# Linear attention into an MLP on one core: q's turn split over two engines, a state term in a bank of its own, state sums in alternation, and another order for one wave's loads, turns and stores

## Chip, cores, metric

The kernel runs on one core of a Trainium2 chip. The metric is the time of one execution on the device in microseconds (us); the numbers of a kernel are medians over runs. Besides the runs there is one profiled execution, whose trace the views below are taken from.

## What is computed

```python
# attention: B=4 batches, H=8 heads, S=768 positions, D=64, blocks of 64
for b in range(nb):
    qb, kb, vb = (q[:, :, sl], k[:, :, sl], v[:, :, sl])
    intra = einsum('bhic,bhjc->bhij', qb, kb) * Dmask      # causal, lam**(i-j)
    intra = einsum('bhij,bhjd->bhid', intra, vb)
    inter = einsum('bhid,bhde->bhie', qb * lam_pow, kv_state)
    out[:, :, sl] = intra + inter
    kv_state = lam_block * kv_state + einsum('bhsd,bhse->bhde', kb * rev_pow, vb)
# MLP on x = out as 3072 rows of 512; w_in 512 x 2048, w_out 2048 x 512
h = x @ w_in
g = h * (1 / (1 + exp(-1.702 * h)))
result = g @ w_out                                          # 3072 x 512, float32
```

## The kernel before

The 768 positions of the four batches are worked through in six waves of 512 rows. Waves 0 and 1 are made differently from waves 2 to 5: each takes two batches (c = 0 and c = 1) and 256 positions of each, as two blocks of 128 positions interleaved in pairs. Waves 2 to 5 take 128 positions of all four batches. After a wave's attention its rows `xT` go through the MLP, whose products are done in a seven-product scheme (Strassen's) on sums of blocks: `product(w, n, ...)` for the second matrix, `in_product` for the first from wave 1 on.

The order of all engines' instructions is written out by hand (`tc.manual_schedule()`), so each engine's queue has the order of the program text. TensorE interleaves the MLP of one wave with the attention of the next. The steps of that interleaving have short names: `P50` is product 5 of the second matrix, first half of the tokens; `o` and `u` are the sums on VectorE (or from it) that finish two of the output blocks and store them; `p4h` is the last part of product 4. The change lies where wave 0's last products and wave 1's attention meet. Before, the order there on TensorE was: eight transposes of k (c = 0), `p4h`, eight transposes of q, `P50`, scores, the first state sum, `P51`, `d_even`, k's transposes (c = 1), `P30`, output sums, state sums, q's transposes (c = 1), `P31`, then wave 1's MLP with the scores of c = 1 in it.

What the names mean there:

- `turn_pe` (L235 on) transposes a cast k or q with TensorE into a PSUM bank `ps_t` and copies it to SBUF with the engine that it is given (one copy of 1024 columns, or of 512 with a group `g`). `turn_dma` (L246 on) does it by a DMA transpose issued by SyncE; waves 2 to 5 use it.
- `do_cast` multiplies a loaded k or q by its powers of lam into bf16, on VectorE or POOL (GpSimd). `cast_v` casts v, half on POOL and half on ACT (ScalarE) in wave 1.
- `d_scores` and `d_masks` make the scores in `ps_s` and mask them on VectorE. `d_out` sums the outputs of both row groups (A: partitions 0 to 63, Z: 64 to 127) in two banks, `oa` and `oz`, and then adds the second half of the state term, which is in row group Z, by `d_inter`.
- `d_even` makes the first half of the state term, in row group A, ahead of `d_out` in the bank that then serves as `oz`. A one-column copy on ACT (`seen`) stands between the two.
- `d_state` sums k'v for one row group; `d_one` does so for a batch's first row group in a new bank, and `d_keep` copies that to SBUF on ACT.
- `end(w, c)` runs `d_out`, the state sums, the copies to `xT` and the state's update. In `end(0, 1)` the first half of the state term already goes to a bank `ow` of its own; ACT copies two quarters of it to `term` and VectorE adds them.

PSUM has eight banks here in two rings: tag `a` with five and tag `mm` with three. A new tile takes the ring's next bank and waits until its last use is over. Bank X holds the running sum of products 1, 6, 5 and 3, and ACT or VectorE copies it out between them (L486, L484, L495, L500).

SyncE issues nearly all loads, stores and DMA transposes, in program order, and waits in that order for what each needs. Wave 2's loads are issued by `load(2, "kq")` behind the step `o`: k of both halves, then q of both, into one buffer each. Their casts on POOL and their turns come in the loop over wave 1's MLP, behind the stores of the steps `u` and `P31`.

Of the kernel before, what the change touches and what calls it, by code (L numbers as in the profile page):

```python
# [25 lines left out]
def kernel(  # L26
# [13 lines left out]
    nc = tc.nc  # L40
    f32 = mybir.dt.float32
    bf16 = mybir.dt.bfloat16
    B, H, S, D = q.shape
    P = 128
    NP = H // 2
# [27 lines left out]
    HF = 2  # L73
# [41 lines left out]
    A, Z = slice(0, 64), slice(64, P)  # L115
# [119 lines left out]
    def turn_pe(w, c, nm, copy=act_copy, g=None):  # L235
        x = cast[w, c, nm]
        rr = list(range(NP)) if g is None else [2 * g, 2 * g + 1]
        t = acc("ps_t", bf16, [P, len(rr), 2, P])
        for i, r in enumerate(rr):
            for a in range(2):  # L240
                nc.tensor.transpose(t[:, i, a, :], x[:, r, a, :], ident)  # L241
        if g in (None, 0):
            trans[w, c, nm] = work.tile([P, 2 * NP, P], bf16, tag=f"{nm}T{c}", bufs={"k": 1, "q": 2}[nm], name=f"{nm}T")
        copy(trans[w, c, nm][:, 2 * rr[0] : 2 * rr[0] + 2 * len(rr)], t.rearrange("p r a s -> p (r a) s"))
# [31 lines left out]

    kept = {}

    def d_state(w, c, t, bs):
        ks, vt = cast[w, c, "k"], v_sb[w % 2]  # L280
        for p in range(NP):
            for a in range(2):
                for j, js in enumerate((A, Z)):
                    h = 4 * (p // 2) + 2 * j + p % 2
                    nc.tensor.matmul(t[js, p, :], ks[bs, p, a, j * D : j * D + D], vt[bs, 2 * c + a, h, :],  # L285
                                     start=((bs is A or (w, c) in kept) and p + a == 0), stop=(a == 1), skip_group_check=True)

    states, whole = {}, {}

    def d_one(w, c, tag="a"):  # L290
        states[w, c] = t = acc("ps_kv", shape=[P, NP, D], tag=tag)
        d_state(w, c, t, A)

    def d_keep(w, c):
        nc.scalar.copy(kv_sb[1][:, 2 * w + c], states[w, c])
# [13 lines left out]
    def d_even(w, c, tag="a"):  # L309
        whole[w, c] = acc("ps_o", tag=tag)  # L310
        d_inter(w, c, whole[w, c], 0, True)
        nc.scalar.copy(seen, whole[w, c][:, 0, 0:1])
# [18 lines left out]
    def d_x(w, c, i, t, copy):  # L331
        n0 = (2 * c + i) * P
        copy(xT[w][:, :, n0 : n0 + P], t)
# [324 lines left out]
    with tc.manual_schedule():  # L658
        for x, i in ((k_pow, i_k), (q_pow, i_q)):
            nc.scalar.activation(x, ln_lam.unsqueeze(1).to_broadcast([P, 2, H]), EXP, scale=i)  # L660
        mk_pow(inv_pow, -1.0 * P)
        for j, rows in enumerate((A, Z)):
            nc.scalar.activation(blk_pow[rows].rearrange("p (r i) -> p r i", i=2),
                                 ln_lam[rows].rearrange("p (r j i) -> p r j i", i=2, j=2)[:, :, j, :], EXP, scale=1.0 * P)
        nc.scalar.activation(warm, q_pow[:, 0, 0:1], GELU)
        for nm, copies in (("k", (dve_copy, act_copy)), ("q", (act_copy, dve_copy))):
            for g in range(2):
                do_cast(0, 0, nm, nc.vector, g)
            for g in range(2):
                turn_pe(0, 0, nm, copies[g], g)  # L670
                fill(1 + g if nm == "k" else 1 - g)
        gate_pool(loaded[0, 0, "q"][0:1, H // 2, 0:1])
        load_w_in(0)
        load_one(0, 1, "v", v)
        cast_v(0, 0, (act_copy, act_copy))
        for pp in range(2):
            d_scores(0, 0, pp)
            d_masks(0, 0, pp)
        fill(3)
        do_cast(0, 1, "k", nc.gpsimd, 0)  # L680
        for j in range(1, len(IN_CH)):
            load_w_in(j)
        d_one(0, 0, "mm")
        d_keep(0, 0)
        turn_pe(0, 1, "k", act_copy, 0)
        oa, oz = d_out(0, 0, ("mm", "mm"))
        nc.scalar.copy(seen, oz[:, 3, P - 1 : P])
        do_cast(0, 1, "q", nc.vector, 0)
        do_cast(0, 1, "k", nc.vector, 1)
        do_cast(0, 1, "q", nc.vector, 1)  # L690
        turn_pe(0, 1, "q", act_copy, 0)
        d_inter(0, 0, oz, 0, False)
        turn_pe(0, 1, "k", act_copy, 1)
        d_state(0, 0, states[0, 0], Z)
        turn_pe(0, 1, "q", dve_copy, 1)
        d_x(0, 0, 0, oa, act_copy)
        d_x(0, 0, 1, oz, act_copy)
        cast_v(0, 1, (act_copy, pool_copy))
        for j in range(NCH):
            load_w_out(j)  # L700
        for pp in range(2):
            d_scores(0, 1, pp)
            d_masks(0, 1, pp, split=(1,) if pp else ())
        nc.gpsimd.affine_select(mask, mask, pattern=[[0, 1], [1, P]], channel_multiplier=-1, base=0,
                                compare_op=mybir.AluOpType.is_ge, fill=0.0)
        gate_sync(w_out_sb[1][0:1, 0, 0:2])
        load(1)
        mlp1_half(0, 0, 0)
        d_one(0, 1)
        d_keep(0, 1)  # L710
        act_copy(kv_sb[0][:, 0], states[0, 0])

        def scores(w, c):
            for pp in range(2):
                d_scores(w, c, pp)
            for pp in range(2):
                d_masks(w, c, pp)

        def end(w, c):
            oa, oz = d_out(w, c)  # L720
            t = acc("ps_kv", shape=[P, NP, D]) if w else states[w, c]
            if w == 0:
                ow = acc("ps_o", tag="mm")
                d_inter(w, c, ow, 0, True)
                term = work.tile([P, 2, P], f32, tag="sm", bufs=8, name="term")
                nc.scalar.copy(term, ow[:, 0::2])
                d_x(w, c, 0, oa, act_copy)
                n0 = (2 * c + 1) * P
                nc.vector.tensor_copy(xT[w][:, 1::2, n0 : n0 + P], oz[:, 1::2])
                nc.vector.tensor_tensor(xT[w][:, 0::2, n0 : n0 + P], term, oz[:, 0::2], op=ADD)  # L730
            d_state(w, c, t, Z)
            if w and c == 0:
                d_one(w, 1)
            if w:
                d_x(w, c, 0, oa, act_copy)
                d_x(w, c, 1, oz, act_copy if c else dve_copy)
            if w:
                nc.vector.tensor_tensor(kv_sb[0][:, 2 * w + c], kept[w, c], t, op=ADD)
            else:
                nc.scalar.copy(kv_sb[0][:, 2 * w + c], t)  # L740
            if w and c == 0:
                d_keep(w, 1)

        def steps(w, names):
            for s in names.split():
                one_step(w, s)

        end(0, 1)
        for c, fc in ((0, 2), (1, 0), (1, 2)):
            mlp1_half(0, c, fc)  # L750
        for fc in range(4, FFC):
            mlp1(0, fc)
            steps(0, {5: "I1 I2", 7: "I3", 9: "gl3 gl1 gl2 gl4", 11: "W01234", 13: "W11234"}.get(fc, ""))
        steps(0, "p1a gh3 gh1 p2a p7a W23124 p4a p1b p2b gh2 gh4 p7b p4b W33124 p1h p2h p7h")
        do_cast(1, 0, "k", nc.vector, 0)
        do_cast(1, 0, "k", nc.gpsimd, 1)
        do_cast(1, 0, "q", nc.vector)
        steps(0, "p6l p6h")
        turn_pe(1, 0, "k", act_copy)
        steps(0, "p4h o")  # L760
        turn_pe(1, 0, "q", act_copy)
        load(2, "kq")
        cast_v(1, 0, (pool_copy, act_copy))
        do_cast(1, 1, "k", nc.gpsimd)
        steps(0, "P50")
        scores(1, 0)
        d_one(1, 0)
        d_keep(1, 0)
        steps(0, "P51")
        d_even(1, 0, "mm")  # L770
        turn_pe(1, 1, "k", act_copy)
        do_cast(1, 1, "q", nc.gpsimd)
        cast_v(1, 1, (act_copy, pool_copy))
        steps(0, "P30")
        end(1, 0)
        steps(0, "u")
        turn_pe(1, 1, "q", act_copy)
        steps(0, "P31")
        halves = [(c, fc) for c in range(HF) for fc in HALVES]
        for i, (c, fc) in enumerate(halves):  # L780
            if i == 1:
                scores(1, 1)
                d_even(1, 1)
            if i == 3:
                end(1, 1)
            if i == 4:
                x_sums(1)
            mlp1_half(1, c, fc)
            if i == 2:
                steps(0, "I0")  # L790
            if i in (1, 2, 3, 4):
                nm = "kq"[(i - 1) % 2]
                do_cast(2, (i - 1) // 2, nm, nc.gpsimd)
                turn_dma(2, (i - 1) // 2, nm)
            if i == 6:
                load(2, "v")
        steps(1, STEPS[1])
        for w in range(ND, NW):
            steps(w, STEPS[w])
# [30 lines left out]
```

## Time and profile before

| | |
|---|---|
| median of 3 runs | 191.46 us (191.4 to 192.05) |
| profiled execution | 192.02 us, span 190.3 us |
| TensorE matmuls | 183.5 us busy, 96% of the span |
| VectorE | 152.5 us, 80% |
| ACT | 129.9 us, 68% |
| POOL | 53.2 us, 28% |
| clock granted to TensorE | 1.0 of full speed |
| DMA | 33.91 MB, mean 178 GB/s |

The span is what the trace covers; the execution's own time has 1.7 us around it. Busy time of TensorE counts matmuls whose ends are modelled and overlap. In the rows that follow PE is TensorE's matmuls, PEld its weight loads, DVE is VectorE, SPq SyncE's queue of DMA issues, and L with a number is a line of the kernel before.

### The profile page before, as it was taken

How to read it: one execution, taken by the hardware profiler on the slowest of the kernel's cores; microseconds unless marked ns; L12 is line 12 of the kernel's file. 1: busy time of each engine (PE TensorE's matmuls, PEld its weight loads, DVE VectorE, ACT ScalarE, POOL GpSimd, SP SyncE). 2: the span in 40 equal slices, each digit the busy share in tenths (PEclk: the TensorE clock that was granted, in tenths of full speed). 3: DMA queues.
4: the chain of work that ended last, by engine and by line, in shares of the span. 5: the costliest groups of instructions: out<-in, count | busy, mean ns of one | idle time of the engine just before them, and what ended most of it. 6: DMA issues, size and time to landing. Idle time of an engine off the chain costs nothing.

```text
span 190.3 us, 5531 instructions
## 1 busy us (share of the span) xinstructions
PE 183.5 (96%) x2295; PEld 151.5 (80%) x2295; DVE 152.5 (80%) x282; ACT 129.9 (68%) x242; POOL 53.2 (28%) x72
## 2 busy tenths in 40 slices
PE   7889999999999999999999999999999999999993
PEld 2457646888888888888888888888888888888882
DVE  2687697986687799879799879799789797888950
ACT  6677765157777986288895388885488876597611
POOL 5498100246449000294000393000492000000000
PEclk9999999999999999999999999999999999999999
DMA  5999999998987899987899465999355903300113
GB/s 156 303 259 183 205 206 207 314 320 238 238 218 177 194 225 232 227 187 137 200 237 241 156 165 119 232 235 256 134 138 124 209 1 114 110 5 0 55 56 113
DMA packets 90127, 33.91 MB, mean 178 GB/s; under 512 B 67958, under 2 KB 89974, under 8 KB 90102
## 3 DMA queue, kind: packets, MB, share of 16 engines
q1 hardware_dynamic: 84676, 28.84, 60.2%
q0 software_dynamic: 5424, 4.72, 15.2%
q8 instruction: 18, 0.29, 0.6%
q14 instruction: 7, 0.06, 0.1%
q10 hardware_dynamic: 2, 0.00, 0.0%
HBM read 27.26 MB, written 6.29 MB: 176 GB/s over the span
## 4 chain that ended last, share of the span: by engine, by line
PE 90%; SPq 3%; DMA 3%; ACT 1%; DVE 1%; issue 0%; ACTq 0%
PE ps_X L470 22%; PE ps_hX L561 17%; PE ps_V L470 10%; PE ps_hV L561 8%; PE ps_Q L470 6%; PE ps_h L420 6%; PE ps_h L408 5%; PE ps_hQ L561 4%; SPq L84 3%; DMA qf<-in_q_dram 3%; PE ps_s L341 2%; PE ps_o L396 2%; PE ps_o L383 1%; PE ps_o L322 1%; PE ps_t L241 1%; PE ps_kv L285 1%
## 5 line engine op out<-in xcount | busy, mean ns | idle before, releaser
L470 PEld LDWEIGHTS <-g_s 128*128 128x128 bf16 x384 | 37.0, 98 | 4.8
L580 ACT ACTIVATE g_sb<-h_sb 128x512 bf16<-128x512 f32 x54 | 32.6, 631 | 1.2 <-DVE h_sb L569 1.2
L561 PEld LDWEIGHTS <-w_in_t 128*128 128x128 bf16 x288 | 28.2, 98 | 3.3
L470 PEld LDWEIGHTS <-g_sb 128*128 128x128 bf16 x288 | 27.5, 98 | 4.1
L224 ACT COPY part<-ps_hX 128x512 f32<-128x512 f32 x32 | 18.3, 587 | 11.4 <-PE ps_hX L561 11.4
L470 PE MATMUL ps_X<-w_out_t,g_s 128*128 128x256 bf16 x192 | 23.1, 273 | 0.0
L561 PEld LDWEIGHTS <-w_in 128*128 128x128 bf16 x216 | 21.1, 98 | 2.4
L561 PE MATMUL ps_hX<-x_s,w_in_t 128*128 128x256 bf16 x144 | 21.6, 272 | 0.0
L447 DVE TENSOR_TENSOR g_s<-g_sb 128x1024 bf16<-128x1024 bf16 x24 | 16.2, 686 | 5.8 <-ACT g_sb L580 5.6
L212 POOL TENSOR_TENSOR qs<-qf,q_pow 128x512 bf16<-128x512 f32 x16 | 16.6, 1062 | 3.4 <-DMA qf<-in_q_dram 3.4
L212 POOL TENSOR_TENSOR ks<-kf,k_pow 128x512 bf16<-128x512 f32 x16 | 16.3, 1041 | 3.5 <-DMA kf<-in_k_dram 3.5
L653 POOL CAST behind_q<-x_s 1x1 f32<-1x1 bf16 x3 | 0.5, 177 | 57.9 <-DVE x_s L546 57.9
L221 DVE COPY part<-ps_hV 128x512 f32<-128x512 f32 x18 | 12.4, 687 | 5.3 <-PE ps_hV L561 5.3
L486 ACT COPY part<-ps_X 128x512 f32<-128x512 f32 (+1 forms) x13 | 6.7, 518 | 13.0 <-PE ps_X L470 13.0
L569 DVE TENSOR_TENSOR h_sb<-part,ps_hX 128x512 f32<-128x512 f32 x18 | 12.2, 680 | 2.6 <-PE ps_hX L561 2.1
L569 DVE TENSOR_TENSOR h_sb<-part,ps_hV 128x512 f32<-128x512 f32 x18 | 12.3, 684 | 1.0 <-PE ps_hV L561 1.0
L470 PE MATMUL ps_X<-w_out,g_sb 128*128 128x256 bf16 x96 | 12.6, 273 | 0.0
L470 PE MATMUL ps_Q<-w_out,g_sb 128*128 128x256 bf16 x96 | 12.5, 273 | 0.0
L224 ACT CAST v_sb<-vf 128x1024 bf16<-128x1024 f32 (+1 forms) x13 | 11.4, 885 | 1.4 <-DMA vf<-in_v_dram 1.3
L569 DVE TENSOR_TENSOR h_sb<-part,ps_hQ 128x512 f32<-128x512 f32 x18 | 12.2, 679 | 0.0
L580 ACT ACTIVATE g_sb<-ps_hX 128x512 bf16<-128x512 f32 x18 | 10.6, 588 | 1.8 <-PE ps_hX L561 1.8
L470 PE MATMUL ps_V<-w_out_t,g_s 128*128 128x256 bf16 x96 | 11.8, 273 | 0.0
(117 smaller groups left out, 355.8 us busy)
## 6 DMA issues: line engine op xcount, KB each, us to landing
kf<-in_k_dram SPq DMA_DIRECT2D x10, 512.0 KB, 6.6
qf<-in_q_dram SPq DMA_DIRECT2D x10, 512.0 KB, 6.7
vf<-in_v_dram SPq DMA_DIRECT2D x10, 512.0 KB, 6.0
out_dram<-o_sb SPq DMA_DIRECT2D x24, 128.0 KB, 2.4
out_dram<-o_sb SPq DMA_DIRECT2D x12, 256.0 KB, 2.8
w_out<-in_moe_w_out_dram POOLq DMA_DIRECT2D x4, 512.0 KB, 14.2
kf<-in_k_dram SPq DMA_DIRECT2D x4, 256.0 KB, 3.2
qf<-in_q_dram SPq DMA_DIRECT2D x4, 256.0 KB, 5.0
```

Of the source, the lines that this page charges most:

```text
L84: (nc.gpsimd if w == 0 and c and nm == "v" else nc.sync).dma_start(out=x[:, h : h + n], in_=src[2 * w + c, h : h + n, 0 : 2 * P, :].rearra ...
L212: eng.tensor_tensor(x.rearrange("p b (r i j d) -> p j (b r) i d", i=2, j=2, d=D)[:, j], f.rearrange("p h (a d) -> p (h a) d", a=2).rearran ...
L221: nc.vector.tensor_copy(out, in_)
L224: nc.scalar.copy(out, in_)
L408: nc.tensor.matmul(h, w_in_sb[j][:, kc, i * P : (i + 1) * P], xT[w][:, kc, :], start=(kc == 0), stop=(kc == KC - 1))
L420: nc.tensor.matmul(h[:, u, :], w_in_sb[j][:, kc, i * P : (i + 1) * P], xT[w][:, kc, cols], start=(kc == 0), stop=(kc == KC - 1))
L447: nc.vector.tensor_tensor(o, x, y, op=f)
L470: nc.tensor.matmul(bank[:, t], x[:, m, t * P : (t + 1) * P], y, start=((n in (1, 2, 7) or own) and t == ts[0] * last and m == 0), stop=(m ...
L486: nc.scalar.copy(part[w, n, t.start][:, t], bank[:, t])
L561: nc.tensor.matmul(bank[:, u], z[:, kc], y[:, kc], start=(n in (1, 2, 7) and u + kc == 0), stop=(kc == 1), skip_group_check=True)
L569: nc.vector.tensor_tensor(h, h_part[w, g, {2: 1, 5: 7, 4: 6}[n]], bank, op=ADD)
L580: nc.scalar.activation(g_of[w][:, a : b + 1 : b - a, 256 * i : 256 * i + 256], bank, GELU)
```

## The change

The turn of q (c = 0) of wave 1 becomes two groups, one copied by ACT and one by VectorE, and the step `o` moves behind it. In `end(1, 0)` the first half of the state term goes to its own bank `ow` behind `d_out`, with the copies that `end(0, 1)` has, and `d_even(1, 0)` goes. `d_state` takes several sums and alternates their matmuls; `end(1, 0)` runs c = 0's second row group and c = 1's first in one such call. Wave 2's loads come as k, q, k, q. The casts and turns of its first half move ahead of `u` and so ahead of the stores of `u` and `P31`; the second half's stay in the loop.

```diff
-    def d_state(w, c, t, bs):
-        ks, vt = cast[w, c, "k"], v_sb[w % 2]
+    def d_state(w, *sums):
+        vt = v_sb[w % 2]
         for p in range(NP):
             for a in range(2):
-                for j, js in enumerate((A, Z)):
-                    h = 4 * (p // 2) + 2 * j + p % 2
-                    nc.tensor.matmul(t[js, p, :], ks[bs, p, a, j * D : j * D + D], vt[bs, 2 * c + a, h, :],
...
+                for c, t, bs in sums:
+                    for j, js in enumerate((A, Z)):
+                        h = 4 * (p // 2) + 2 * j + p % 2
+                        nc.tensor.matmul(t[js, p, :], cast[w, c, "k"][bs, p, a, j * D : j * D + D],
+                                         vt[bs, 2 * c + a, h, :],
...
         def end(w, c):
             oa, oz = d_out(w, c)
             t = acc("ps_kv", shape=[P, NP, D]) if w else states[w, c]
-            if w == 0:
+            if c == (w == 0):
                 ow = acc("ps_o", tag="mm")
                 d_inter(w, c, ow, 0, True)
                 term = work.tile([P, 2, P], f32, tag="sm", bufs=8, name="term")
...
-            d_state(w, c, t, Z)
             if w and c == 0:
-                d_one(w, 1)
-            if w:
+                states[w, 1] = acc("ps_kv", shape=[P, NP, D])
+                d_state(w, (c, t, Z), (1, states[w, 1], A))
+            else:
+                d_state(w, (c, t, Z))
+            if w and c:
                 d_x(w, c, 0, oa, act_copy)
-                d_x(w, c, 1, oz, act_copy if c else dve_copy)
+                d_x(w, c, 1, oz, act_copy)
...
         turn_pe(1, 0, "k", act_copy)
-        steps(0, "p4h o")
-        turn_pe(1, 0, "q", act_copy)
-        load(2, "kq")
+        steps(0, "p4h")
+        turn_pe(1, 0, "q", act_copy, 0)
+        turn_pe(1, 0, "q", dve_copy, 1)
+        steps(0, "o")
+        for c in range(HF):
+            load_one(2, c, "k", k)
+            load_one(2, c, "q", q)
...
         steps(0, "P51")
-        d_even(1, 0, "mm")
         turn_pe(1, 1, "k", act_copy)
...
         end(1, 0)
+        for nm in "kq":
+            do_cast(2, 0, nm, nc.gpsimd)
+            turn_dma(2, 0, nm)
         steps(0, "u")
...
-            if i in (1, 2, 3, 4):
-                nm = "kq"[(i - 1) % 2]
-                do_cast(2, (i - 1) // 2, nm, nc.gpsimd)
-                turn_dma(2, (i - 1) // 2, nm)
+            if i in (1, 2):
+                do_cast(2, 1, "kq"[i - 1], nc.gpsimd)
+                turn_dma(2, 1, "kq"[i - 1])
```

More of the change, by code (lines that the diff above doesn't have):

```diff
@@ L277 @@
     kept = {}
-    def d_state(w, c, t, bs):
-        ks, vt = cast[w, c, "k"], v_sb[w % 2]
+    def d_state(w, *sums):
+        vt = v_sb[w % 2]
         for p in range(NP):
             for a in range(2):
-                for j, js in enumerate((A, Z)):
-                    h = 4 * (p // 2) + 2 * j + p % 2
-                    nc.tensor.matmul(t[js, p, :], ks[bs, p, a, j * D : j * D + D], vt[bs, 2 * c + a, h, :],
-                                     start=((bs is A or (w, c) in kept) and p + a == 0), stop=(a == 1), skip_group_check=True)
+                for c, t, bs in sums:
[3 more added lines that the diff above has]
+                                         vt[bs, 2 * c + a, h, :],
+                                         start=((bs is A or (w, c) in kept) and p + a == 0), stop=(a == 1),
+                                         skip_group_check=True)
     states, whole = {}, {}
@@ L291, in d_one @@
         states[w, c] = t = acc("ps_kv", shape=[P, NP, D], tag=tag)
-        d_state(w, c, t, A)
+        d_state(w, (c, t, A))
     def d_keep(w, c):
@@ L693 @@
         turn_pe(0, 1, "k", act_copy, 1)
-        d_state(0, 0, states[0, 0], Z)
+        d_state(0, (0, states[0, 0], Z))
         turn_pe(0, 1, "q", dve_copy, 1)
```

## The prediction, made before the result

> **What bounds the kernel now.** I read the busy times and the chain that ended last, then the waits from 57 us on, and then the timeline of the stretch that the change edits, engine by engine.
>
> ```profile
> PE 183.5 (96%) x2295; PEld 151.5 (80%) x2295; DVE 152.5 (80%) x282; ACT 129.9 (68%) x242; POOL 53.2 (28%) x72
> ```
>
> ```profile
> PE 90%; SPq 3%; DMA 3%; ACT 1%; DVE 1%; issue 0%; ACTq 0%
> ```
>
> TensorE is busy for 96% of the span and is 90% of the chain. From 57 us to the end the view of waits has two rows for TensorE's weight loads and none for its matmuls:
>
> ```profile
> PEld L341 <- issue: 1.7, 8, 0.2
> PEld L383 <- issue: 0.8, 4, 0.2
> ```
>
> Both are pauses of 0.2 us ahead of matmuls on half the array's rows, not waits for another engine. So what TensorE gains before 57 us arrives at the end undiminished, and so does what it loses. The change moves nothing before 39 us. The question is what TensorE gains between 39 and 53 us, and whether the moved DMAs still land ahead of their reader. TensorE's timeline there (start, length, what; in brackets the idle time before and who ended it):
>
> ```profile
> 40.68 1.03 PE L470 MATMUL ps_X<-w_out_t,g_s 128*128 128x256 bf16 x8
> 41.97 0.64 PE L262 MATMUL ps_s<-qT,kT 64*64 64x128 bf16 x32 [0.25 <-ACT qT L224]
> 42.41 0.48 PE L285 MATMUL ps_kv<-v_sb,ks 64*64 64x64 bf16 x16
> 42.82 1.05 PE L470 MATMUL ps_X<-w_out_t,g_s 128*128 128x256 bf16 x8
> 43.80 0.30 PE L304 MATMUL ps_o<-qT,kv 64*64 64x128 bf16 x4
> 44.03 0.62 PE L241 MATMUL ps_t<-ident,ks 128*128 128x128 bf16 x8
> 44.55 1.03 PE L470 MATMUL ps_X<-w_out,g_s 128*128 128x256 bf16 x8
> 45.51 0.64 PE L322 MATMUL ps_o<-sm,v_sb 64*64 64x128 bf16 x32
> 45.99 0.28 PE L304 MATMUL ps_o<-qT,kv 64*64 64x128 bf16 x4
> 46.10 0.67 PE L285 MATMUL ps_kv<-v_sb,ks 64*64 64x64 bf16 x32
> 46.70 0.62 PE L241 MATMUL ps_t<-ident,qs 128*128 128x128 bf16 x8
> 47.16 1.04 PE L470 MATMUL ps_X<-w_out,g_s 128*128 128x256 bf16 x8
> 48.03 1.04 PE L420 MATMUL ps_h<-xT,w_in 128*128 128x256 bf16 x8
> 48.99 0.64 PE L262 MATMUL ps_s<-qT,kT 64*64 64x128 bf16 x32
> ```
>
> The rows overlap, because a length includes the last matmul's way to PSUM; what counts is the distance between starts: 0.87 for a product of eight behind which full-array work follows (47.16 to 48.03), 0.46 for eight transposes (46.70 to 47.16).
>
> **The change part by part.** The other engines' timeline in that stretch, and two groups of copies:
>
> ```profile
> 40.90 1.02 ACT L224 COPY qT<-ps_t 128x1024 bf16<-128x1024 bf16 x1
> 41.80 0.63 ACT L224 CAST v_sb<-vf 128x512 bf16<-128x512 f32 x1
> 43.91 0.59 ACT L495 COPY part<-ps_X 128x512 f32<-128x512 f32 x1 [0.33 <-PE ps_X L470]
> 47.75 1.02 ACT L224 COPY qT<-ps_t 128x1024 bf16<-128x1024 bf16 x1
> 40.73 0.69 DVE L502 TENSOR_TENSOR o_sb<-part,ps_Z 128x512 f32<-128x512 f32 x1
> 41.34 0.68 DVE L502 TENSOR_TENSOR o_sb<-part,ps_Q 128x512 f32<-128x512 f32 x1
> 42.42 2.48 DVE L273 TENSOR_TENSOR sm<-ps_s,mask_d 128x512 bf16<-128x512 f32 x4 [0.41 <-PE ps_s L262]
> 41.41 2.04 POOL L204 TENSOR_TENSOR ks<-kf,kd_pow 128x512 bf16<-128x512 f32 x2 [0.89 <-DMA kf<-in_k_dram]
> 45.40 0.61 POOL L218 CAST v_sb<-vf 128x512 bf16<-128x512 f32 x1
> ```
>
> ```profile
> L224 ACT COPY qT<-ps_t 128x512 bf16<-128x512 bf16 x2 | 1.2, 586 | 1.2 <-PE ps_t L241 1.2
> L221 DVE COPY qT<-ps_t 128x512 bf16<-128x512 bf16 x2 | 0.8, 425 | 1.0 <-PE ps_t L241 1.0
> ```
>
> *q's turn by two engines.* The scores of c = 0 wait for ACT's copy of 1024 columns, 40.90 to 41.92. After: ACT copies half of them in 0.586, done at 41.49, which the first 16 matmuls need; VectorE takes the other half behind the Z sum, 41.34 to 41.77, ahead of the second 16. TensorE is then bounded by its own product, which ends at 40.68 + 1.03 = 41.71; a half-array row starts 0.07 ahead of such an end (43.80 against 42.82 + 1.05). Scores start at 41.64 instead of 41.97: 0.33 gained. ACT's cast of v moves up by 0.43 to end at 42.0, so the first state sum follows the scores at 41.64 + 0.44 = 42.08 and the next product, P51, 0.41 later at 42.49. On VectorE the Q sum (step o) now stands behind the copy: the sum starts at about 41.70 (the Z sum of 0.69 lets its successor start 0.08 early, so this copy too), the masks 0.61 behind it at 42.31 instead of 42.42. Masks gain only 0.1 and end at 42.31 + 2.48 = 44.79.
>
> *One row group's term in its own bank.* The four matmuls at 43.80 (d_even) and ACT's touch of their bank go. k's turn follows P51 at once, at 42.49 + 0.87 = 43.36, where it took 44.03 - 42.82 = 1.21. POOL has the last half of that k cast at 41.41 + 2.04 = 43.45, and only the last four transposes need it: no wait. The next product, P30, could start at 43.36 + 0.46 = 43.82. But it adds to bank X, and ACT must first copy P51's result out of it (L495). That copy started 0.04 behind P51's end (42.82 + 1.05 = 43.87), and P30 0.05 behind the copy's end (44.50). After: P51 ends at 43.54, the copy runs from 43.58 to 44.17, P30 starts at 44.22. So P30 stands 0.33 earlier, not 0.73: the second gain is swallowed there. The output sums follow 0.96 later, at 45.18; their masks ended at 44.79. The four matmuls come back behind them, at 0.11 (46.10 - 45.99), so the state sums could start at 45.18 + 0.48 + 0.11 + 0.11 = 45.88. What ACT and VectorE get for it, by wave 0's rows:
>
> ```profile
> L726 ACT COPY term<-ps_o 128x256 f32<-128x256 f32 x1 | 0.4, 372 | 0.2 <-PE ps_o L304 0.2
> L729 DVE CAST xT<-ps_o 128x256 bf16<-128x256 f32 x1 | 0.4, 425 | 0.7 <-PE ps_o L304 0.7
> ```
>
> That is 0.37 more on ACT, and on VectorE this copy and a sum of its shape in place of one copy of all 512 columns. Queued behind the term on ACT are the copy of x, two of the state, and q's second turn (47.75 to 48.77), for which the scores at 48.99 wait. ACT has the 0.33 from P51 and the 0.2 by which those scores trailed their copy to pay with, against 0.37. I take nothing, with up to 0.2 as the other end.
>
> *Sums alternate.* Alternating row groups, as the output sums do already, 32 matmuls take 0.48 (45.51 to 45.99). In sequence they took 0.60 (46.10 to 46.70), and the difference of 0.12 I take for the switch back to full rows, so alternating is worth nothing by these rows, at most 0.1. But the sums of both states now run together, and the seventh matmul already needs the second v, whose cast ends on POOL at 45.40 + 0.61 = 46.01. POOL has been busy since the landing at 41.41, which the change doesn't move. 26 matmuls are left then: 46.06 + 26 x 0.015 + 0.12 = 46.57 for q's turn instead of 46.70. From here on everything follows at the old distances: **0.13 gained**, rounded to 0.15.
>
> The page TensorEngine Tiling of the Trainium skill (Key Properties) says that independent tiles load weights and multiply in parallel, and that a change of tiling mode drains the array. By the first, two row groups in turn would halve the state sums and give some 0.2 more. This trace speaks against it: the output sums alternate and still take 0.48. The drain agrees with the 0.2 of issue above.
>
> *Wave 2's DMAs.* SyncE's and POOL's timeline before, one load's time to landing (the second k, issued at 45.51), and that of the turns:
>
> ```profile
> 41.45 2.73 SPq L508 DMA_DIRECT2D out_dram<-o_sb  x4
> 47.05 5.85 SPq L88 DMA_DIRECT2D qf<-in_q_dram  x2
> 53.00 4.23 SPq L508 DMA_DIRECT2D out_dram<-o_sb  x4
> 61.53 1.26 SPq L248 DMA_TRANSPOSE qT<-qs  x1
> 54.98 2.37 POOL L212 TENSOR_TENSOR qs<-qf,q_pow 128x512 bf16<-128x512 f32 x2 [3.38 <-DMA qf<-in_q_dram]
> 64.94 0.62 PE L341 MATMUL ps_s<-qT,kT 64*128 64x128 bf16 x16
> ```
>
> ```profile
> kf<-in_k_dram SPq DMA_DIRECT2D x1, 512.0 KB, 7.5
> ```
>
> ```profile
> DMA to landing us min/median/max: 2.7/2.7/4.5
> ```
>
> The loads are all issued by 52.90 in either order, and three turns took 57.23 to 61.53, 1.43 each. Before, the last turn starts at 61.53 and lands at 64.2, 0.7 ahead of its reader at 64.94, and TensorE waits for nothing. After, q of c = 0 is the second load; the second landed at 53.0. POOL casts it by 55.1 to 55.4, its turn is issued by 56.5 to 56.8, four stores take between 2.73 and 4.23 (the second with loads still queued), and the last turn starts at 60.7 to 62.5, landing at 63.4 to 65.2. The reader then comes at 64.8. With the loads landed by then I take stores near the low end: hidden, with 1 us in hand, and up to 0.4 lost at the other end. The stores that wait behind turns hold two of eight buffers, and those come round again only in wave 1's output sums, behind these scores.
>
> **Sum.** The profiled execution took 192.02 (span 190.3), 0.56 above the median of 191.46. After: 191.87 for it, and from the median 191.46 - 0.15 = **191.3**.
>
> **Rivals.**
> *Neither ACT's copy nor POOL's cast holds TensorE back.* Then both gains arrive: 0.33 and 0.40, less 0.11 for the four matmuls put back: 0.6, time 190.85. Against it: ACT stood idle for 0.33 ahead of its copy, so that start hangs on P51 and not on ACT's load; and the cast of v comes last in a queue that began with a landing.
> *The added copy on ACT becomes the wait*, and q's second turn ends late for its scores. At 0.2 beyond my sum the gain is gone: 191.5.
> *The last turn of wave 2 lands behind its reader.* If q of c = 0 lands only where the third load did, at 54.98, it is cast by 57.35 and turned by 58.8, stores go to 63.0, the last turn starts at 64.4 and lands at 67.1: TensorE stands 2.3 at its scores, 193.6. It decides where the last turn starts later than 62.1; from there each us is one us of time. For it: two turns now stand behind loads, and stores ahead of the last turns. Against: the cast before was late mainly because q was third in the queue.
> *The change moves instructions without any effect*: 191.46, inside the forecast's own range.
>
> **How the numbers follow.** The forecast with 0 to 0.3 gained (191.15 to 191.45) has 0.55, both gains 0.2, the added copy 0.1, the late turn 0.15, of which a third beyond 1 us. The runs shown spread from 191.4 to 192.05, so a range has to hold part of that: 190.7 to 192.2 leaves out the worst of the late turn and some of the spread. 0.5% is 0.96 us, about what a measurement of this kernel can tell from no change. No gain here reaches it alone, but half of the second case could with the spread of runs: faster 0.1. The late turn, with some spread, gives slower 0.08. Same: 0.82.
>
> **What would show it.** Right: scores of c = 0 at 41.6, P30 at 44.2 just behind ACT's copy, a wait for POOL's v inside the state sums, q's turn at 46.57, and no DMA wait at wave 2's first scores near 64.8. Wrong: P30 or the state sums without those waits, a DMA wait at those scores, or any wait of TensorE behind 57 us that the trace before lacks.

## The result and the profile after

The changed kernel takes 193.32 us (median of 14 runs) against 191.47 for the kernel before (14 runs): ratio 1.0085, 95% interval 1.0066 to 1.0103. The prediction was 191.3, in a range of 190.7 to 192.2, with 0.08 on slower. By that ratio it is slower by 1.6 us (the two medians lie 1.85 apart): outside the range, and by a way that is none of the prediction's cases. The profiled execution took 193.57 (span 191.8), 1.55 above that of before.

First the busy times and the chain that ended last, from the page of the kernel after:

```profile
PE 183.5 (96%) x2295; PEld 151.2 (79%) x2295; DVE 156.3 (82%) x284; ACT 129.6 (68%) x242; POOL 53.2 (28%) x72
PE 82%; DMA 6%; DVE 5%; POOL 2%; issue 1%; ACT 1%; SPq 1%; ACTq 0%; DVEq 0%
```

TensorE and POOL are as busy as before. VectorE is busy for 3.8 us more, with two instructions more, and has gone from 1% of the chain to 5%. The waits of TensorE's matmuls and weight loads from 50 to 64 us, where the kernel before has none on another engine (us in total, times, longest):

```profile
PE ps_hX L564 <- DVE x_s L549: 0.5, 1, 0.5
PE ps_hQ L564 <- DVE h_sb L572: 0.5, 1, 0.5
```
```profile
PEld L564 <- issue: 0.9, 2, 0.6
PEld L564 <- DVE x_s L549: 0.8, 1, 0.8
```

TensorE's timeline there, after:

```profile
57.97 0.60 PE L564 MATMUL ps_hQ<-xT,w_in 128*128 128x256 bf16 x4
59.06 0.61 PE L564 MATMUL ps_hX<-x_s,w_in_t 128*128 128x256 bf16 x4 [0.49 <-DVE x_s L549]
60.39 0.60 PE L564 MATMUL ps_hX<-x_s,w_in_t 128*128 128x256 bf16 x4
61.44 0.60 PE L564 MATMUL ps_hQ<-xT,w_in 128*128 128x256 bf16 x4 [0.46 <-DVE h_sb L572]
66.35 0.62 PE L344 MATMUL ps_s<-qT,kT 64*128 64x128 bf16 x16
```

and before, the same two places:

```profile
57.84 0.60 PE L561 MATMUL ps_hQ<-xT,w_in 128*128 128x256 bf16 x4
58.29 0.60 PE L561 MATMUL ps_hX<-x_s,w_in_t 128*128 128x256 bf16 x4
59.60 0.60 PE L561 MATMUL ps_hX<-x_s,w_in_t 128*128 128x256 bf16 x4
60.04 0.60 PE L561 MATMUL ps_hQ<-xT,w_in 128*128 128x256 bf16 x4
```

The distance from one group of four to the next is 0.44 to 0.45 before. After, it is 1.09 at the first place and 1.05 at the second: 0.64 and 0.61 lost. From q's turn of c = 1 (46.70 before, 46.61 after) to wave 2's first scores (64.94 and 66.35) the whole loss is 19.74 - 18.24 = 1.50, so these two places carry 1.25 of it. Another 0.22 goes just ahead of them, at the first group that reads an `x_s`: it starts 0.66 behind the group before it (56.88 to 57.54), where it was 0.44. Behind wave 2's first scores nothing differs: 1.41 late there, and a span longer by 1.5.

What TensorE waits for first is VectorE's `x_s` (the sums of x that the first products of wave 1 read). The second wait, for `h_sb`, follows from it: VectorE makes `h_sb` behind its last `x_s`, and the copy that leads up to it starts at 60.12 where it started at 58.04. VectorE's and POOL's timeline after:

```profile
52.70 0.29 DVE L540 TENSOR_TENSOR w_in_t<-w_in,w_in_t 128x256 bf16<-128x256 bf16 x1
53.02 1.17 DVE L540 TENSOR_TENSOR w_in_t<-w_in,w_in_t 128x256 bf16<-128x256 bf16 x1
54.11 1.13 DVE L540 TENSOR_TENSOR w_in_t<-w_in 128x256 bf16<-128x256 bf16 x1
55.16 1.13 DVE L540 TENSOR_TENSOR w_in_t<-w_in,w_in_t 128x256 bf16<-128x256 bf16 x1
57.85 1.16 DVE L549 TENSOR_TENSOR x_s<-x_s,xT 128x512 bf16<-128x512 bf16 x1
59.04 1.15 DVE L549 TENSOR_TENSOR x_s<-xT,x_s 128x512 bf16<-128x512 bf16 x1
52.99 2.10 POOL L212 TENSOR_TENSOR qs<-qf,q_pow 128x512 bf16<-128x512 f32 x2 [1.56 <-ACT xT L224]
55.05 2.15 POOL L212 TENSOR_TENSOR ks<-kf,k_pow 128x512 bf16<-128x512 f32 x2
57.64 2.27 POOL L212 TENSOR_TENSOR qs<-qf,q_pow 128x512 bf16<-128x512 f32 x2 [0.44 <-PE ps_hX L564]
```

and VectorE's before:

```profile
53.51 0.28 DVE L537 TENSOR_TENSOR w_in_t<-w_in,w_in_t 128x256 bf16<-128x256 bf16 x1
54.83 0.42 DVE L546 TENSOR_TENSOR x_s<-x_s,xT 128x512 bf16<-128x512 bf16 x1
55.29 1.15 DVE L546 TENSOR_TENSOR x_s<-xT,x_s 128x512 bf16<-128x512 bf16 x1
```

The same instruction takes 0.29 until 52.99 and 1.13 to 1.17 from then on, for as long as POOL casts: one VectorE sum per POOL instruction (2.10 / 2 = 1.05). Before, POOL had nothing to do from 51.6 to 54.98, since it waited for q as the third load, and the eight w_in_t sums ran in that gap. After, q is the second load, and its cast starts at 52.99, in the middle of them. The `x_s` that TensorE waits for ends at 57.85 + 1.16 = 59.01 where it ended at 54.83 + 0.42 = 55.25: 3.76 later. It was needed at 58.29 before, so 3.04 of slack were there, and 0.7 is missing. Of the 3.76, 2.50 come from the w_in_t sums alone (last end 56.29 against 53.79). A sum with one input in PSUM is not held up: the masks take 0.68 in both kernels, and the sum `kv` (L743, L738 before) takes 0.41 beside a cast (56.22 after) and 0.41 with POOL idle (53.72 before).

### The profile page after: what moved, and what is told of

Read it like the earlier page. It is cut to its first block, busy times and chain, and to the rows that moved or that the text cites. A ratio compares the mean times of both kernels' runs of the same rounds, so it can differ in the third digit from the quotient of the medians.

```text
span 191.8 us, 5533 instructions
## 1 busy us (share of the span) xinstructions
PE 183.5 (96%) x2295; PEld 151.2 (79%) x2295; DVE 156.3 (82%) x284; ACT 129.6 (68%) x242; POOL 53.2 (28%) x72
## 4 chain that ended last, share of the span: by engine, by line
PE 82%; DMA 6%; DVE 5%; POOL 2%; issue 1%; ACT 1%; SPq 1%; ACTq 0%; DVEq 0%
PE ps_X L473 22%; PE ps_hX L564 16%; PE ps_V L473 10%; PE ps_hV L564 8%; PE ps_Q L473 6%; PE ps_h L411 5%; PE ps_hQ L564 4%; DMA vf<-in_v_dram 4%; DMA qf<-in_q_dram 2%; PE ps_s L344 2%; PE ps_o L399 2%; PE ps_h L423 2%; DVE w_in_t L540 2%; DVE sm L273 1%; DVE x_s L549 1%; PE ps_o L386 1%
## 5 line engine op out<-in xcount | busy, mean ns | idle before, releaser
L473 PE MATMUL ps_X<-w_out,g_s 128*128 128x256 bf16 x96 | 11.6, 272 | 0.2 <-ACT part L498 0.2
```

The source lines that it names most:

```text
L473: nc.tensor.matmul(bank[:, t], x[:, m, t * P : (t + 1) * P], y, start=((n in (1, 2, 7) or own) and t == ts[0] * last and m == 0), stop=(m ...
```

## The experiments

**Theory A:** POOL's casts hold up VectorE's sums whose two inputs lie in SBUF, and the new order of loads puts a cast onto the w_in_t sums. **Rivals:** the DMA transposes ahead of the stores do it; the edits to wave 1 cost time; a late turn of wave 2.

**Only the order of the loads**, in the kernel before.

```diff
-        load(2, "kq")
+        for c in range(HF):
+            load_one(2, c, "k", k)
+            load_one(2, c, "q", q)
```

> The kernel before, with wave 2's loads as k q k q and nothing else of the change. Theory A (POOL's cast of q, now second to land, starts near 53 us and holds up VectorE's sums on two SBUF tensors): VectorE's w_in_t sums after 53 us take 1.1 us each instead of 0.3, TensorE waits for x_s near 58 us, 192.9 to 193.4. Theory B (the DMA turns, issued at 52.9 in the changed kernel, slow VectorE): turns start at 57 us here, so no loss, 191.5. Theory C (the edits of wave 1 cost it): 191.5.

Ratio 1.0083 (1.006 to 1.0106), 193.52 against 191.93: the loss of the whole change comes from these three lines. VectorE's and TensorE's timeline in this kernel:

```profile
52.62 1.13 DVE L537 TENSOR_TENSOR w_in_t<-w_in,w_in_t 128x256 bf16<-128x256 bf16 x1
59.21 0.60 PE L561 MATMUL ps_hV<-x_s,w_in_t 128*128 128x256 bf16 x4 [1.68 <-DVE x_s L546]
```

Five sums from 52.62 on take 1.02 to 1.13 each, and TensorE stands 1.68 for `x_s`. In this kernel the first DMA transpose starts only at 56.14, when three of the five sums are over, so the transposes are not what holds them.

**Only the edits to wave 1** (split turn, own bank, alternating sums); loads, casts and turns of wave 2 as before.

> Wave 1's edits alone (q's turn split, own bank, alternating sums); loads k k q q, casts and turns where they stood before. Theory A and theory B: 191.2 to 191.4, a gain of 0.1 to 0.2, with VectorE's w_in_t sums at 0.3 us each. Theory C: the loss stays, 193.3.

Ratio 1.000 (0.9977 to 1.0024). All eight w_in_t sums take 0.28 to 0.33, and TensorE waits for no `x_s`. The edits to wave 1 cost nothing, and gain nothing that can be told.

**One POOL cast of the kernel before, done twice.**

```diff
-            for j in range(2):
+            for j in (0, 1, 0, 1) if (w, c, nm) == (2, 0, "k") else (0, 1):
```

> The kernel before, with POOL's cast of wave 2's first k done twice (two more instructions of 1.05 us, in POOL's idle time from 51.6 to 53.7 us); no DMA moves. Theory A: VectorE's w_in_t sums from 51.9 us on are held up to 1.1 us each while POOL casts, 192.5 to 193.3. Theory B and theory C: 191.5.

Ratio 1.0195 (1.0152 to 1.0237): two instructions of 1.05 on an engine that is busy for 28% of the span cost 4 us. The extra casts run until 53.52, and sums beside them take 0.46 and 1.02. But in the traced execution q's own cast also starts earlier, at 53.94 where the kernel before had 54.98, and POOL then casts until 60.39; four more sums take 1.02 to 1.15 there, and TensorE waits 1.68 and 0.62 for `x_s`. So the trace doesn't tell how much of the loss is the extra casts' own. That there is one, the times tell: all six executions (194.04 to 196.71) lie above the longest of the 23 of the kernel before (193.12). It is more than expected, and a part of it is the clock, by the view of windows (busy of PE, PEld, DVE, ACT, POOL with counts; granted clock; DMA share; GB/s):

```profile
58.00:59.00 1.00, 0.00 (x0) 0.00 (x0) 1.00 (x3) 0.53 (x2) 1.00 (x2) 1.00 1.10 251
60.00:61.00 1.00, 0.57 (x6) 0.27 (x3) 0.97 (x2) 0.00 (x0) 0.39 (x1) 0.94 0.71 160
61.00:62.00 1.00, 0.81 (x4) 0.58 (x5) 0.96 (x3) 0.00 (x0) 0.00 (x0) 0.50 1.07 240
63.00:64.00 1.00, 1.00 (x7) 0.69 (x6) 0.03 (x1) 0.89 (x2) 0.00 (x0) 0.50 0.40 88
```

From 61 to 64 TensorE got half its clock, and its groups of four stand 0.83 to 0.85 apart instead of 0.44. Four of the six executions have a mean clock of 0.989 to 0.991 (195.97 to 196.71), the other two 1.0 (194.04 and 195.21): against the median of 191.93 those two lose 2.1 and 3.3 us without it.

**The cure: the changed kernel with the eight sums moved away from wave 2's casts.** The sums of step I0 go into two gaps on VectorE, four ahead of `end(1, 0)` and four behind `u`; `in_sums` gets an argument for it, which isn't shown.

```diff
         steps(0, "P30")
+        in_sums(0, (0,))
         end(1, 0)
...
         steps(0, "u")
+        in_sums(0, (1,))
...
-            if i == 2:
-                steps(0, "I0")
```

> The changed kernel, with the eight w_in_t sums of group 0 moved into VectorE's idle stretches at 44.8 and 47.8 us, ahead of POOL's casts of wave 2. Theory A: only the x_s sums still meet POOL's casts (1.15 us each), and they end in time: 191.1 to 191.4. Theory B: the same x_s sums meet the turns, and some loss may stay, 191.3 to 192. Theory C: 193.3.

Ratio 0.9985 (0.996 to 1.0009): the loss is gone, with loads, casts and turns of the change all in place. `x_s` still meets POOL, but has time now:

```profile
54.29 1.16 DVE L549 TENSOR_TENSOR x_s<-x_s,xT 128x512 bf16<-128x512 bf16 x1
55.48 1.15 DVE L549 TENSOR_TENSOR x_s<-xT,x_s 128x512 bf16<-128x512 bf16 x1
```

It ends at 56.63, and from 50 to 64 us TensorE's matmuls wait for no engine. It isn't shown to be faster than the kernel before: the interval reaches over 1. The new place isn't free of POOL either. Two of the four sums ahead of `end(1, 0)` meet wave 1's casts: one takes 1.02 beside q's, and this one starts 0.12 behind POOL's copy of v, which has a single input in SBUF and takes 0.67:

```profile
44.89 0.69 DVE L540 TENSOR_TENSOR w_in_t<-w_in 128x256 bf16<-128x256 bf16 x1
```

**Does any work on POOL hold VectorE up, or only work that reads SBUF?** The kernel before, with four memsets on POOL behind k's first cast, into a tile that is overwritten later.

```diff
                 do_cast(2, (i - 1) // 2, nm, nc.gpsimd)
+                if i == 1:
+                    for g in (0, 1, 0, 1):
+                        nc.gpsimd.memset(trans[1, 0, "k"][:, 4 * g : 4 * g + 4], 0.0)
```

> The kernel before with four extra memsets on POOL behind its first cast of wave 2's k, from about 51.6 us on, where POOL was idle until q's landing at 54.98 and VectorE made the w_in_t sums in 0.28 each; nothing reads what they write before it is written again. Theory A in its narrow form (only a POOL instruction that reads from SBUF holds up a VectorE sum with two inputs from SBUF): the sums stay at 0.28 to 0.3 and the time stays at the level of before, 0.2% at most. Wide form (any POOL instruction does): sums beside the memsets take as long as a memset, 0.6 or more, and if the memsets cover all eight sums, x_s ends 2 or more us later and TensorE waits up to 1.5: 192.5 to 193.5. If the memsets run past 54.98, q's cast and with it the last x_s start later by that much in both forms.

Ratio 0.9997 (0.9978 to 1.0016): the narrow form holds. The traced execution is a long one (194.89, where the median is 191.85), so only what lies side by side in it is read:

```profile
52.09 1.92 POOL L796 MEMSET kT<- 128x512 bf16 x4
53.26 0.28 DVE L537 TENSOR_TENSOR w_in_t<-w_in,w_in 128x256 bf16<-128x256 bf16 x1
54.52 2.24 POOL L212 TENSOR_TENSOR qs<-qf,q_pow 128x512 bf16<-128x512 f32 x2 [0.52 <-DVE w_in_t L537]
54.72 1.14 DVE L537 TENSOR_TENSOR w_in_t<-w_in 128x256 bf16<-128x256 bf16 x1
```

Beside a memset a sum takes 0.28; beside a cast, half a microsecond later, 1.14. The page SBUF — State Buffer of the Trainium skill (Who interferes with whom) says just this: a VectorE instruction with two SBUF inputs contends with a GpSimd instruction that reads SBUF, not with one that only writes, and the one that comes second waits for the whole instruction of the other. The traces agree in all three points. On the third: the `x_s` of the kernel before that starts at 54.83, ahead of POOL's cast, takes 0.42 and the cast 2.37, where the casts behind it take 2.05.

**The changed kernel with the loads as before** (k k q q), turns still ahead of the stores. This also comes near the prediction's rival of the late turn, which needs q of c = 0 to land where the third load did, at 54.98, and the last turn to start later than 62.1.

> The changed kernel with wave 2's loads in the order k, k, q, q as before; casts and turns of the first half stay ahead of the stores. Theory A: q of c = 0 lands as third load at about 55, POOL is idle from 51.6 to 55, VectorE's eight w_in_t sums run at 0.3 each and x_s is in time; the loss of the changed kernel (1.6) is gone: 191.3 to 191.7, as far as the second turn isn't late. The prediction's rival of the late turn: q is cast by 57.4, turned by 58.8, four stores take until about 62, the last turn starts at 63 to 64.4 and lands at 65.6 to 67.1, behind its reader at 64.8 to 65: TensorE waits 0.8 to 2.3 at wave 2's first scores, 192.3 to 193.8. If neither is so (the loads' order is not what hurts), the time stays at the changed kernel's 193.3 with w_in_t sums of 1.1.

Ratio 1.0013 (0.9985 to 1.0041): the loss goes with the order of the loads alone.

```profile
53.11 0.28 DVE L540 TENSOR_TENSOR w_in_t<-w_in,w_in_t 128x256 bf16<-128x256 bf16 x1
54.06 2.42 POOL L212 TENSOR_TENSOR qs<-qf,q_pow 128x512 bf16<-128x512 f32 x2 [2.88 <-DMA qf<-in_q_dram]
61.99 1.26 SPq L248 DMA_TRANSPOSE qT<-qs  x1
64.54 0.75 PE L344 MATMUL ps_s<-qT,kT 64*128 64x128 bf16 x16
```

The last w_in_t sum is over when q is cast. The first DMA transpose is issued at 51.84 here, and the sums beside it still take 0.28, so the transposes ahead of the stores hold none of them up. The last turn starts at 61.99, earlier than the 63 to 64.4 expected, because q landed by 54.06 and the four stores took 2.63, the low end of the prediction's bounds. That is 0.1 short of the rival's own condition. With 2.7 to its landing the turn is there at 64.69, while the scores that start at 64.54 are under way: they take 0.13 longer than after (0.75 against 0.62), and the next product starts 0.68 behind them instead of 0.56. The view of waits names nothing for so short a time; that it is the turn is an inference. So the rival came to its edge here and cost about 0.1; a turn that starts later was not tried.

**v first on POOL**, on top of the cure: the second half of v (c = 1) is cast ahead of q, so that the state sums need not wait for it.

```diff
-        do_cast(1, 1, "q", nc.gpsimd)
         cast_v(1, 1, (act_copy, pool_copy))
+        do_cast(1, 1, "q", nc.gpsimd)
```

> The changed kernel with the eight sums for the next wave's first product moved as in the run before (into VectorE's gaps around wave 1's c = 0), and on POOL the cast of the second half of v (c = 1) ahead of the cast of q (c = 1). Theory A (the loss is VectorE's two-input sums held up by POOL's casts; the wave-1 edits gain what was worked out): the state sums no longer wait for POOL's v, 0.44 in the run before; q's cast ends 0.6 later, but its turn comes behind all state sums, so about 0.1 to 0.2 is gained, 191.5 to 191.8, hardly above what can be told. Rival (POOL's casts of c = 1 bound wave 1 from the landing on): q's cast then ends later than its turn wants it, TensorE waits for POOL's q in place of POOL's v, and nothing is gained: the distance from POOL's start on k (c = 1) to q's turn stays 5.2, time 191.8 to 192.0.

A miss for both: ratio 1.0103 (1.0074 to 1.0132), 193.82. Its trace was of the shortest run (192.29) and showed 0.41 and 0.57 of new waits, so the same kernel was run again for a second trace:

> The same kernel as the run with the sums moved and v cast ahead of q on POOL, for a second trace: its times were 192.3 to 194.7 and the trace was of the shortest. If the 1.5 that its trace did not show lie in wave 1 (q's later cast lengthens TensorE's wait at q's turn, and VectorE's sums meet POOL's q cast), a trace of a run near 193.8 has q's turn of c = 1 at 8.5 or more behind k's turn of c = 0 (8.06 in the first trace); if they lie at wave 2, the distance from k's turn to wave 2's first scores grows (26.73 in the first) with q's turn unmoved and a wait of TensorE near x_s or those scores.

193.66, ratio 1.0097 (1.0058 to 1.0136), traced at 193.02:

```profile
45.91 1.12 DVE L540 TENSOR_TENSOR w_in_t<-w_in,w_in_t 128x256 bf16<-128x256 bf16 x1
48.12 0.38 ACT L301 COPY half<-ps_kv 128x256 f32<-128x256 f32 x1 [1.60 <-DVE kv L743]
44.13 0.67 POOL L218 CAST v_sb<-vf 128x512 bf16<-128x512 f32 x1 [1.31 <-DVE sm L273]
44.76 2.13 POOL L204 TENSOR_TENSOR qs<-qf,qd_pow 128x512 bf16<-128x512 f32 x2
46.95 0.40 PE L241 MATMUL ps_t<-ident,qs 128*128 128x128 bf16 x4 [0.65 <-POOL qs L204]
49.46 0.64 PE L262 MATMUL ps_s<-qT,kT 64*64 64x128 bf16 x32 [0.37 <-ACT qT L224]
```

POOL stands 1.31 ahead of v. The releaser named is VectorE's masks, but v's load was issued at 37.7 and took 6.3 to land by the profile's count, which is 44.0: v comes last of the loads, and POOL, put in front of it, idles while q lies ready. TensorE then waits for q in two steps (0.31 and 0.65) and for ACT's copy of it. q's turn stands 46.95 - 38.27 = 8.68 behind k's, as expected for a longer run. The rival was right in kind (POOL's q takes the place of POOL's v) and far too low in size. ACT's copy is late for the reason that this document is about: POOL's casts of v and q now lie beside the moved sums, three of the first four take 0.58, 1.12 and 1.12, VectorE's `kv` behind them starts 9.36 behind k's turn (8.43 in the cure), and ACT stands 1.60 for it ahead of q's copy. The last of the other four takes 1.14 beside the cast of wave 2's k, so the masks come late too, and TensorE stands 0.29 for them. From k's turn to wave 2's first scores it is 27.56 (26.73 in the first trace, 26.22 in the cure, 25.65 in the kernel before), and 0.62 of the 0.83 more than in the first trace lies at q's turn (8.68 against 8.06).

**The edits to wave 1, the split turn alone and two pairs**, on the kernel before. A single execution of the split turn alone took 190.43; it was then run 12 times, with the two pairs beside it.

> The kernel before with only q's turn (wave 1, c = 0) copied by two engines and step o behind it. By the prediction's steps: scores of c = 0 start 0.33 earlier beside k's turn than before, the product behind the first state sum as well, k's turn of c = 1 too, and the product P30 follows ACT's copy of bank X 0.33 earlier; with no alternation of the sums there is no wait for POOL's second v, and q's turn of c = 1 comes 0.3 earlier: 191.2. Rival (POOL's casts bound this stretch): POOL's q or v holds q's turn, which comes 0.1 earlier at most: 191.4. One look can't tell those times apart; the trace can.

> Again the kernel before with only q's turn (wave 1, c = 0) copied by two engines and step o behind it, now timed. The trace of the first look had q's turn of c = 1 7.02 behind k's turn of c = 0, where the kernel before has 7.41, and the same 0.39 at wave 2's first scores. If that is the edit's worth, the time is before's less 0.4: 191.1 to 191.3, ratio 0.998. If the look's 190.4 was its spread: ratio 1.000.

> The kernel before with the split turn and the state term of c = 0 in its own bank, but the state sums one after the other; loads, casts and turns of wave 2 as before. By the prediction's steps the bank brings nothing more, since the product P30 waits for ACT's copy of bank X: P30 0.33 earlier beside k's turn (4.93 where before had 5.26), q's turn of c = 1 7.0 to 7.1 behind k's, time as with the split alone, 191.1 to 191.4. Rival (it is the bank that costs the split's gain, by the term's copy on ACT and the longer addition): q's turn at 7.2 or later, or its scores waiting for ACT's copy, 191.5 to 191.8.

> The kernel before with the bank and the alternating sums, q's turn copied by ACT alone as before. By the prediction's steps P30 stands where it stood (5.26 behind k's turn), held by the copy of bank X, and the alternating sums wait for POOL's second v; q's turn comes 7.3 to 7.4 behind k's, time as before, 191.4 to 191.6. Rival (the two edits cost by themselves): q's turn at 7.5 or later, 191.7 to 192.

Over 12 runs each, the split turn alone has 1.0021 (0.9996 to 1.0047), split and bank 1.0016 (0.9995 to 1.0038), bank and alternation 1.0006 (0.9985 to 1.0026): none can be told from no change, and 190.43 lies just below the spread of the 12 (190.67 to 193.36). The traces of two executions of the split kernel show why one trace doesn't settle it. In the first, q's turn (c = 1) starts 7.02 behind k's turn of c = 0 (38.07 to 45.09). In the second it is 7.75 (38.16 to 45.91):

```profile
39.85 1.03 PE L470 MATMUL ps_X<-w_out_t,g_s 128*128 128x256 bf16 x8 [0.19 <-DVE part L484]
45.57 0.41 PE L285 MATMUL ps_kv<-v_sb,ks 64*64 64x64 bf16 x14 [0.21 <-POOL v_sb L218]
45.91 0.62 PE L241 MATMUL ps_t<-ident,qs 128*128 128x128 bf16 x8
52.73 1.16 DVE L537 TENSOR_TENSOR w_in_t<-w_in,w_in_t 128x256 bf16<-128x256 bf16 x1
```

The second has a wait for VectorE's copy out of bank X, which the pair without the split turn has too (0.20), and one for POOL's v inside the sums. The split turn does save its 0.33 beside the product ahead of it (scores 0.97 and 0.96 behind P50, where before had 1.29), but what follows hangs on when POOL begins its casts of c = 1: 2.03 behind k's turn in the first, 2.76 in the second, and that is the whole difference. Split and bank had 7.33, not the 7.0 to 7.1 expected, and P30 at 5.13, not 4.93; bank and alternation had 7.43 with P30 at 5.25, about as expected (7.3 to 7.4, 5.26).

The second execution also shows the held-up sums in a kernel with the old order of loads. q's cast starts at 52.69 there, and the last sum takes 1.16; TensorE later stands 0.46 for `h_sb`. In the long execution of the memset run it stands 0.68 for `x_s` and 0.46 for `h_sb`. What decides is the distance from the first w_in_t sum to q's cast, since the eight sums need 1.93 alone. It is 1.22 in the changed kernel and 0.72 with the loads alone; in the nine traces with the old order it goes from 1.26 to 3.38, with 3.12 in the kernel before. So the old order kept the two apart in six of those nine executions and not in the memset run, the doubled cast and this one, and the kernel before's slack is that of one execution.

## Why the prediction was wrong, step by step

*What bounds the kernel: right.* TensorE is the bound, and what it loses before 57 us, or right behind it, reaches the end undiminished in the traced execution: 1.41 at wave 2's scores, 1.5 in the span. The text's own test for being wrong, a wait of TensorE behind 57 us that the trace before lacks, is what the trace shows, twice.

*The steps of wave 1: right but for one bound, and too small to count.* The kernel after has

```profile
41.70 0.64 PE L262 MATMUL ps_s<-qT,kT 64*64 64x128 bf16 x32
44.24 1.03 PE L473 MATMUL ps_X<-w_out,g_s 128*128 128x256 bf16 x8 [0.23 <-ACT part L498]
46.27 0.41 PE L286 MATMUL ps_kv<-v_sb,ks 64*64 64x64 bf16 x26 [0.25 <-POOL v_sb L218]
46.61 0.62 PE L241 MATMUL ps_t<-ident,qs 128*128 128x128 bf16 x8
```

where 41.64, 44.22 behind ACT's copy, a wait for POOL's v with 26 matmuls left, and 46.57 were foreseen: the second gain is swallowed by bank X, as worked out, and 0.09 of the forecast 0.13 arrives. One bound of that step was wrong: alternation was taken as worth nothing, 0.1 at most, by the 0.48 of the output sums. Their matmuls are of 64x128, though, and those of the state sums of 64x64, so that row is no bound for them. In the first run with v ahead of q, where no wait for v stands in the sums, the trace has

```profile
45.33 0.47 PE L286 MATMUL ps_kv<-v_sb,ks 64*64 64x64 bf16 x32
45.73 0.40 PE L241 MATMUL ps_t<-ident,qs 128*128 128x128 bf16 x4
```

which is 0.40 for the 32 alternating sums, where 0.60 was the distance in sequence: 0.2 saved, as the prediction worked it out from the Trainium skill's rule that independent tiles work in parallel (the page TensorEngine Tiling (Array Packing), Key Properties). The trace sides with the page there, with a third saved and not a half. In the changed kernel the wait for v hides it, and in the pair of bank and alternation the distance is 0.63, with v cast only 0.24 behind the sums' start. But the split kernel's 7.02 and 7.75 show that a single execution moves such a distance by 0.7, so the agreement to 0.06 is partly luck, and the sum of 0.15 is not to be seen in the times (1.000, 0.9977 to 1.0024). The rival with both gains at 0.6 is out by the same interval, just: 0.6 would be a ratio of 0.997.

*Wave 2's DMAs: the step that failed.* The loads, casts and turns came as worked out (the last turn starts at 61.40, within 60.7 to 62.5, and lands in time), and the step ended with "hidden". It followed POOL's earlier cast of q forward to its turn, its stores and its reader, and never asked what else runs while POOL casts. There is no term for VectorE in it. Yet the trace of before had the row: `x_s` at 55.29, 0.3 behind the start of POOL's cast at 54.98, took 1.15, and the one ahead of it 0.42. Carried over to the w_in_t sums, that row gives an estimate: a cast 2 us earlier meets three more of them, at about 1.15 instead of 0.29, and that is 2.6 us, with `x_s` on top, against 3.04 of slack. Measured were 1.13 to 1.17, 2.50 us, and 1.26 on `x_s`. The order of loads alone does all of it (1.0083), and either undoing it (1.0013) or moving the sums (0.9985) removes it.

*The rivals.* The late turn carried all of the text's chance for slower and did not happen in the changed kernel; with the loads in the old order it came to the edge of its condition and cost about 0.1. The added copy on ACT cost nothing: the scores of c = 1 start 0.97 behind the product ahead of them, where it was 0.96. That both gains arrive is out, since P30 waits 0.23 for ACT's copy of bank X. The case that came was missing.

## What to carry to other kernels

When an instruction is moved earlier, look at what the other engines do in the stretch that it moves into, and not only at who waits for its result: two engines that share no data can still hold each other up. A group of instructions whose mean hides two durations (0.28 and 1.13 for one shape) is the sign; sort it by what else ran at the time. An engine at 28% can cost time by when it works, and a gap on it may be what keeps another engine in time. Whether such a gap is there can change from execution to execution, so one trace without the collision doesn't show that it never happens.

## What the hardware showed that was not expected

A VectorE sum of 128x256 with both inputs in SBUF takes 0.28 us alone, 0.28 beside a POOL memset, and 1.02 to 1.17 beside POOL casts of 1.05 each; a sum of 128x512 goes from 0.42 to 1.15. A sum that starts 0.12 behind a POOL copy of 0.67 takes 0.69. So a held-up sum costs about what POOL's instruction costs, whatever the sum's size.

In the run with the doubled cast, TensorE's clock fell to 0.50 for 3 us after two waits of 1.68 and 0.62. The page TensorE: Matmul & The Clock Gate of the Trainium skill (What's actually happening) gives half rate after at least one idle window of about 3.4 us. Here only 58 to 59 us was wholly idle, with 0.57 busy in 60 to 61, and the clock fell all the same. In the kernel with only the loads reordered, a single wait of 1.68, with 58 to 59 us wholly idle too, left the clock at 1.00.
